# A fused Mamba-2 scan and gated feed-forward kernel: two one-element products take over waits ahead of the first state sums, and the mask products of chunk 1 are cut differently

## The chip, the core and the metric

The kernel runs on one core of a Trainium2 chip. A core has a matrix engine (TensorE, PE in the profile, with its weight loads listed as PEld), a vector engine (VectorE, DVE), an activation engine (ScalarE, ACT), a general engine (GpSimd, POOL) and an engine that issues transfers (SyncE, SP). Each runs its own list of instructions in order; they meet at semaphores. Matrix products write to PSUM, eight banks of accumulators per partition, and transfers between HBM and the on-chip memory go through 16 DMA engines.

The metric is the device time of one execution in microseconds. The kernel before has a median of 341.88 us over three runs (340.96 to 342.74).

## What is computed

A state-space scan over 4 batches, 8 heads and 768 positions, and on its output, seen as 3072 tokens of 256 features, a feed-forward block with a hard-swish gate:

```python
for c in range(nc):
    cum = np.cumsum(log_a[:, :, sl], axis=-1)
    L = np.exp(cum[:, :, :, None] - cum[:, :, None, :]) * causal
    M = np.einsum('bhin,bhjn->bhij', Cc, Bc) * L
    y[:, :, sl] = M @ xc + (Cc @ state) * np.exp(cum)
    state = decay_full * state + sum_j(Bc_j xc_j * decay_from_j)
h = x @ w_in                        # 3072 x 256 by 256 x 2048
g = h * np.clip(h + 3.0, 0.0, 6.0) / 6.0
out = g @ w_out                     # 2048 back to 256
```

The weights arrive as 64-bit floats and are turned into 32-bit ones on the chip.

## The kernel before

The sequence is cut into six chunks of 128 positions (`NC`), and each chunk into two halves of 64 (`HT`). All four batches of a chunk are done together, so a chunk is 512 tokens for the feed-forward block. The order of the work is written out by hand: the statements at the end of the kernel function are recorded in that order, each engine gets its instructions in it, and semaphore waits are put in where an instruction needs another engine's result, a transfer, or a PSUM bank that is still being read. Nothing is moved after that.

The change lies in the opening, before the first feed-forward product. In order of the program:

- `diff_mask` (L385) fills PSUM banks with the causal mask: a product of an identity matrix `ident_h` with `hide`, a 128x64 tile that is 0 where a position may be seen and a large negative number where not. For chunk 0 the four batches use banks f0 to f3, one product of 512 columns each. For chunk 1 batches 0 and 1 use the two banks "o", batches 2 and 3 the banks y0 and y1; there the bank of 8 heads is filled in 2 products for batch 0 and in 4 for the others. `mask_again` (L401) writes three of chunk 0's banks once more. These products depend only on constants and run while VectorE and ScalarE make the cumulative logarithms.
- `diff_less` (L407) and `diff_pick` (L413) add the differences of the cumulative logarithms to the masks, once VectorE has split them into three bf16 parts (L330). `diff_exp` (L422) is ScalarE's exponential of such a bank, which gives the decay matrix `L` in on-chip memory and frees the bank.
- `ends` (L451) is GpSimd's product of B with the decay at a half's end: the tile `bs`. `scores` (L569) multiplies C with B on TensorE.
- `own_banks(0)` takes the banks y0 and y1 for chunk 0's output and state sums. They held the masks of chunk 1, batches 2 and 3, so they come free with the last two exponentials of `diff_exp(1, ...)`.
- `into_state(0, 0, 1)` (L592) makes the state sums: 32 products of `bs` and `xt` in tiles of 64 rows by 32 columns (L601). The first waits for three things: a ScalarE instruction (the bank), a GpSimd instruction (`bs` of batch 0), and the transfer of `xt`, which `load_x(0)` issues on SyncE's queue at L132. An instruction carries one wait here, so the other two stand on a separate wait instruction in TensorE's list in front of it.
- `multiply(0)` copies the sums out of PSUM (`take`, L617, and L627 on ScalarE) and scales `L` by the scores on VectorE (L632). `mix(0)` (L668) makes the output of chunk 0: products of `xt` with `L` (L680) and of the state (L556). `keep(0)` copies it to `yT` (L696).
- Between these, `weights(0, n)` are pieces of the decoding of the first weights: L246, L270 and L273 on ScalarE, L249, L253, L263, L265, L277 and L287 on VectorE.
- Then `mlp_in` begins the feed-forward block of chunk 0: L706 runs 16 column blocks of two fp32 products each through four PSUM banks, with the ramp on ScalarE (L809) and its product on VectorE (L814). The later chunks use products split in three parts (L770) and follow without a pause.

An fp32 product takes two passes, each with its weight load and its product in the trace; a bf16 one takes a single pass, and its weight load is an instruction of its own in the program.

Of the kernel before, what the change touches and what calls it, by code (L numbers as in the profile page):

```python
# [21 lines left out]
def kernel(  # L22
# [24 lines left out]
    nc = tc.nc  # L47
    P = 128
    NB, NH, S, D = x.shape
# [114 lines left out]
    ident = const.tile([P, P], FP32, name="ident")  # L164
    make_identity(nc, ident)
    ident_h = const.tile([P, P], BF16, name="ident_h")
    hide = const.tile([P, HT], BF16, name="hide")
    nc.gpsimd.memset(hide, 0.0)

    def conceal_in(t, pattern):  # L170
# [23 lines left out]
        out=head, in_=head, pattern=[[-2 * N, NQ], [-N, 2]], compare_op=ALU.is_ge,  # L194
        fill=0.0, base=0, channel_multiplier=1)
    nc.gpsimd.affine_select(
        out=head, in_=head, pattern=[[2 * N, NQ], [N, 2]], compare_op=ALU.is_ge,
# [183 lines left out]
    ys, cbs, sps, adds = {}, {}, {}, {}  # L381
# [3 lines left out]
    def diff_mask(c, b):  # L385

        if c == 0:
            d = ps.tile([P, NH, HT], FP32, name="d", tag=f"f{b}")
        elif b < 2:
            d = ps_o.tile([P, NH, HT], FP32, name="d", tag="o")  # L390
        else:
            d = ps_y.tile([P, NH, HT], FP32, name="d", tag=f"y{b % 2}")
        n = NH if c else NH // (2 if b == 0 else 4)
        for h in range(0, NH, n):
            nc.tensor.matmul(  # L395
                out=d[:, h:h + n], lhsT=ident_h,
                rhs=hide.unsqueeze(1).to_broadcast([P, n, HT]), start=(h == 0), stop=True,
                skip_group_check=True)
        ds[c, b] = d
# [169 lines left out]
    def scores(c):  # L569

        bT, cT, _ = bTs[c]
        cbs[c] = [ps.tile([P, NB, 2, HT], FP32, name="cb", tag=f"f{q}") for q in range(NQ)]
        if c not in ys and c:
            own_banks(c)
        for b in range(NB):
            for a, rows in enumerate(HALF):  # L580
                for q in range(NQ):
                    pair = slice(32 * q, 32 * q + 32)
                    nc.tensor.matmul(  # L583
                        out=cbs[c][q][rows, b], lhsT=bT[pair, b, rows],
                        rhs=cT[pair, b, :, rows], start=(b == 0), stop=True,
                        tile_position=(32 * q, a * HT), skip_group_check=True)
        if c == TURN:
            from_state(c, 0)
        if 0 < c <= TURN:
            into_state(c, *range(1 if c == TURN else 2))  # L590

    def into_state(c, *halves):  # L592
        xt, bs = xts[c], bss[c]
        own = c > TURN, c >= TURN
        if c > TURN:
            sps[c][0] = ps.tile([P, NB, 2 * D], FP32, name="sp", tag="f3")
        for b in range(NB):
            for q in range(NQ):
                hs = slice(b * NH + 2 * q, b * NH + 2 * q + 2)
                for a in halves:  # L600
                    nc.tensor.matmul(  # L601
                        out=sps[c][a][32 * q:32 * q + 32, b],
                        lhsT=bs[HALF[a], hs].rearrange("s h n -> s (h n)"),
                        rhs=xt[HALF[a], hs].rearrange("s h d -> s (h d)"),
                        start=(b == 0 and (c == 0 or own[a])), stop=True,
                        tile_position=(a * HT, 32 * q), skip_group_check=True)
# [32 lines left out]
    def sums(c):  # L639

        if c < NC - 1:
            own_halves(c, 1)
            sps[c][1] = ys[c].pop("more")
        if c == TURN:
            into_state(c, 1)
            return
        into_state(c, *range(2 if c < NC - 1 else 1))
        mids[c] = att.tile([P, NB, 2 * D], FP32, name="mid", bufs=1)
        new_state(mids[c], sps[c][0], tmps[c])
# [500 lines left out]
    for c in range(2):  # L1150
        for b in range(NB):
            diff_mask(c, b)
# [49 lines left out]
    for k in range(NC):  # L1202
        gTs[k] = ffn.tile([P, NF, TB], FP32, name="gT")
        c, ahead = k + 1, k + 2
# [194 lines left out]
```

## Time and profile before

| | us |
|---|---|
| median of three runs | 341.88 (340.96 to 342.74) |
| the profiled execution | 340.38 |
| its span, from the first to the last instruction | 338.6 |
| its mean granted TensorE clock | 0.983 of full speed |

The profile is of one execution. Its page gives the busy time of each engine, the granted clock over the span, the queues of the transfers, and the chain of work that ended last; the trace behind it can be asked for the instructions of a stretch of time, for the waits of an engine, for one line or tile, and for the busy time in windows. Each waiting time is put down to the semaphore that came last by the profile's own reckoning, and "issue" stands where an engine waited for nothing that the profile knows. The duration of a matrix product is modelled; its start is measured. In a list, "x64" counts instructions that follow one another, and the time beside it covers them all.

Below is the page's second part, the span in 40 slices of 8.5 us. A digit is the busy share in tenths; PEclk is the granted clock of TensorE in tenths.

```
PE   7789999999999999999999999999999999999995
PEld 4564448888878888888888888888888888899995
DVE  7769999869789729968958657947768958599974
ACT  3858887657986752488653378634488212677661
POOL 2100000062365596269984068781048750000000
PEclk9959999999999999999999999999999999999999
DMA  6869981392990205229207239100132001110001
```

The first three slices, up to 25 us, hold the opening. TensorE has its only gaps there, apart from the very end, and in the third slice its clock is at half.

### The profile page before, as it was taken

To read this page: it belongs to the slowest core of one execution; us is meant where nothing else is said; L and a number is where in the kernel's file an instruction comes from. 1 tells how busy PE (TensorE), PEld (TensorE's weight loads), DVE (VectorE), ACT (ScalarE), POOL (GpSimd) and SP (SyncE) were. 2 spreads that over 40 slices of the span, in tenths; PEclk is the share of its full clock that TensorE was granted. 3 is DMA by queue.
4 is the path that set the end of the run, shared out by engine and by line. 5 is a ranking of instruction groups with operands and counts; after the bars stand their busy time and mean duration, and the time that the engine had idled before them with its cause. 6 is when DMAs were issued, how large, how long until landed. Compare 5 with 4: busy or idle time off the path is not lost.

```text
span 338.6 us, 8337 instructions
## 1 busy us (share of the span) xinstructions
PE 329.6 (97%) x3361; PEld 266.6 (79%) x3361; DVE 263.1 (78%) x419; ACT 208.3 (62%) x450; POOL 129.1 (38%) x126
## 2 busy tenths in 40 slices
PE   7789999999999999999999999999999999999995
PEld 4564448888878888888888888888888888899995
DVE  7769999869789729968958657947768958599974
ACT  3858887657986752488653378634488212677661
POOL 2100000062365596269984068781048750000000
PEclk9959999999999999999999999999999999999999
DMA  6869981392990205229207239100132001110001
GB/s 105 172 199 313 133 298 42 102 140 59 200 121 0 50 17 128 56 34 105 55 2 161 34 60 84 43 2 9 28 62 30 2 4 17 27 21 0 2 0 62
DMA packets 90277, 25.22 MB, mean 74 GB/s; under 512 B 82880, under 2 KB 86624, under 8 KB 89728
## 3 DMA queue, kind: packets, MB, share of 16 engines
q1 hardware_dynamic: 89664, 24.57, 38.3%
q8 instruction: 26, 0.43, 0.5%
q10 hardware_dynamic: 576, 0.13, 0.2%
q14 instruction: 11, 0.09, 0.1%
HBM read 21.33 MB, written 3.29 MB: 73 GB/s over the span
## 4 chain that ended last, share of the span: by engine, by line
PE 97%; ACT 1%; issue 0%; POOL 0%; DVE 0%; POOLq 0%
PE h L770 33%; PE wb L1018 9%; PE h L706 9%; PE wc L1018 8%; PE o L827 8%; PE wa L1018 8%; PE o_end L982 6%; PE y L680 3%; PE wb L1026 3%; PE y L556 2%; PE cb L583 2%; PE d L395 1%; PE d L417 1%; PE y L601 1%; PE d L408 1%; PE o_end L1000 1%
## 5 line engine op out<-in xcount | busy, mean ns | idle before, releaser
L814 DVE SCALAR_TENSOR_TENSOR gT<-gT,h 128x512 f32<-128x512 f32 x96 | 64.7, 683 | 22.8 <-ACT gT L809 21.4
L809 ACT ACTIVATE gT<-h,half 128x512 f32<-128x512 f32 x96 | 65.6, 685 | 25.1 <-PE h L770 21.3
L790 ACT ACTIVATE h<-h 128x512 f32<-128x512 f32 x66 | 38.2, 585 | 37.2 <-PE h L770 37.0
L770 PE MATMUL h<-y_hi,w_part 128*128 128x512 f32 x160 | 51.5, 407 | 0.0
L770 PE MATMUL h<-y_less,w_part 128*128 128x512 f32 x160 | 50.0, 399 | 0.0
L770 PE MATMUL h<-y_lo,w_part 128*128 128x512 f32 x160 | 49.5, 395 | 0.0
L873 POOL TENSOR_TENSOR s<-gT 128x512 f32<-128x512 f32 x16 | 25.3, 1583 | 50.0 <-DVE gT L814 50.0
L770 PEld LDWEIGHTS h<-y_lo,w_part 128*128 128x128 f32 x160 | 30.0, 188 | 7.3
L770 PEld LDWEIGHTS h<-y_hi,w_part 128*128 128x128 f32 x160 | 30.0, 188 | 6.9 <-DVE gT L814 0.3
L770 PEld LDWEIGHTS h<-y_less,w_part 128*128 128x128 f32 x160 | 29.1, 188 | 6.1 <-DVE h L787 0.2
L445 ACT ACTIVATE L<-L,cum_n 128x64 f32<-128x64 f32 x128 | 31.7, 337 | 1.1 <-POOL L L173 1.1
L706 PE MATMUL h<-yT,w_in 128*128 128x512 f32 x64 | 30.0, 633 | 0.0
L827 PE MATMUL o<-w_out,gT 128*128 128x256 f32 x128 | 28.8, 381 | 0.0
L827 PEld LDWEIGHTS o<-w_out,gT 128*128 128x128 f32 x128 | 24.1, 190 | 3.8 <-issue 0.5
L706 PEld LDWEIGHTS h<-yT,w_in 128*128 128x128 f32 x64 | 13.0, 205 | 16.3 <-issue 15.0
L873 POOL TENSOR_TENSOR gT<-gT 128x512 f32<-128x512 f32 x16 | 23.9, 1501 | 0.7
L173 POOL TENSOR_SCALAR_AFFINE_SELECT L<-L 64x1024 f32<-64x1024 f32 (+1 forms) x16 | 18.7, 1178 | 7.3 <-DMA L<-cum_d 7.0
L910 DVE TENSOR_TENSOR q_part<-gT,q_part 128x256 fp32r<-128x256 f32 x24 | 21.4, 922 | 0.0
L982 PE MATMUL o_end<-v_pair,g_pair 128*128 128x256 f32 x120 | 21.1, 281 | 0.0
L873 POOL TENSOR_TENSOR s<-s,gT 128x512 f32<-128x512 f32 x16 | 20.6, 1293 | 0.0
L982 PEld LDWEIGHTS o_end<-v_pair,g_pair 128*128 128x128 f32 x120 | 18.8, 189 | 1.2
L456 POOL TENSOR_TENSOR bs<-B,L 128x128 f32<-128x128 f32 x24 | 10.6, 462 | 19.3 <-ACT L L445 13.9
(166 smaller groups left out, 616.9 us busy)
## 6 DMA issues: line engine op xcount, KB each, us to landing
raw<-in_moe_w_in_dram SPq DMA_DIRECT2D x4, 1024.0 KB
raw<-in_moe_w_out_dram SPq DMA_DIRECT2D x4, 1024.0 KB
L<-cum_d SPq DMA_DIRECT2D x8, 512.0 KB
xt<-in_x_dram SPq DMA_DIRECT2D x6, 512.0 KB
out_dram<-back SPq DMA_DIRECT2D x128, 16.0 KB
B<-in_B_dram SPq DMA_DIRECT2D x6, 256.0 KB
eto<-cum_e SPq DMA_DIRECT2D x20, 64.0 KB
pairs<-in_C_dram SPq DMA_DIRECT2D x36, 32.0 KB
```

Source lines behind the costliest of these rows:

```text
L173: nc.gpsimd.affine_select(out=t[rows], in_=t[rows], pattern=pattern, compare_op=ALU.is_ge, fill=-1e5, base=base, channel_multiplier=-1)
L445: nc.scalar.activation(Ls[c][:, b, h], Ls[c][:, b, h], AF.Exp, bias=cum_n[:, c, g:g + 1])
L706: nc.tensor.matmul(out=h[:, t:t + n], lhsT=w_in[f // FP][:, j, f % FP * P:(f % FP + 1) * P], rhs=yTs[k][:, j].rearrange("p b i -> p (b i)" ...
L770: nc.tensor.matmul(out=hs_[k, f], lhsT=w[j][:, f % FP * P:(f % FP + 1) * P], rhs=y[:, j], start=(start and j == 0), stop=True, skip_group_ ...
L790: nc.scalar.activation(h, h, AF.Copy, scale=1.0 / EPS + 1.0)
L809: nc.scalar.activation(gTs[k][:, f], h, AF.Relu, bias=half, scale=1.0 / 6.0)
L814: nc.vector.scalar_tensor_tensor(out=g, in0=g, scalar=1.0, in1=h, op0=ALU.min, op1=ALU.mult)
L827: nc.tensor.matmul(out=o[:, b % 2], lhsT=gTs[0][:, f, b * P:(b + 1) * P], rhs=w_out[:, f], start=(f == 0 and b % 2 == 0), stop=True, skip_ ...
L873: nc.gpsimd.tensor_tensor(out=o, in0=p_, in1=q_, op=op)
L910: nc.vector.tensor_tensor(out=l[:, j], in0=g[:, j], in1=h[:, j].bitcast(FP32), op=ALU.subtract)
L982: nc.tensor.matmul(out=ends_["cross" if n == 2 else "squares"][b], lhsT=g_parts[t][n][:, b * P:(b + 1) * P], rhs=w, start=(t == 0 and b < ...
L1018: nc.tensor.matmul(out=bank[:, slot], lhsT=lhs[:, j], rhs=rhs[:, j], start=(clear and j == 0), stop=True, skip_group_check=True)
```

## The change

In `diff_mask` the banks of chunk 1 are filled in one product for batch 0 and in two for batch 1, where there were two and four; batches 2 and 3 keep four. This removes three weight loads and three products of TensorE's first instructions, with the same columns written.

In `into_state`, for chunk 0 alone, two products of one element each come before the sums. Both write to the first element of the bank that the sums start afresh, so their results are discarded. The first multiplies a column of `ident_h` with a column of `hide` (bf16); it is the first to write the bank, so it takes the wait on ScalarE's exponential. The second multiplies a column of `bs` with a column of `ident` (fp32); it takes the wait on GpSimd. The first state sum then has only the wait on the transfer of `xt`, and the separate wait instruction in front of it is no longer there.

```diff
@@ diff_mask
-        n = NH if c else NH // (2 if b == 0 else 4)
+        n = NH if c else NH // (1 if b == 0 else 2 if b == 1 else 4)
         for h in range(0, NH, n):
@@ into_state
         if c > TURN:
             sps[c][0] = ps.tile([P, NB, 2 * D], FP32, name="sp", tag="f3")
+        if c == 0:
+            one = sps[c][0][:1, 0, :1]
+            for left, right in ((ident_h[:, :1], hide[:, :1]), (bs[:, 0, :1], ident[:, :1])):
+                nc.tensor.matmul(
+                    out=one, lhsT=left, rhs=right, start=True, stop=True, skip_group_check=True)
         for b in range(NB):
```

TensorE's list then differs in these places alone; the lists of the other engines and the queues are the same, instruction by instruction and wait by wait:

```
before                                             after
two products d<-hide,ident_h of 256 columns        one of 512 columns
four products d<-hide,ident_h of 128               two of 256
eight products d<-hide,ident_h of 128              eight of 128
...
                                                   weight load ident_h
                                                   product y<-hide,ident_h 1x1   waits ACT
                                                   product y<-ident,bs 1x1       waits POOL
first L601, waits DMA, ACT, POOL                   first sum, waits DMA
```

## The prediction

> **What bounds the kernel now.** I read the page's busy shares and chain first, then the list of whom TensorE waited for.
>
> ```profile
> span 338.6 us, 8337 instructions
> PE 329.6 (97%) x3361; PEld 266.6 (79%) x3361; DVE 263.1 (78%) x419; ACT 208.3 (62%) x450; POOL 129.1 (38%) x126
> PE 97%; ACT 1%; issue 0%; POOL 0%; DVE 0%; POOLq 0%
> ```
>
> TensorE (PE) is busy 97% of the span and carries 97% of the chain that ends last. So time is won or lost where PE stands idle or runs slowly. The list of its waits is complete in four lines (total, times, longest):
>
> ```profile
> PE d L395 <- POOL head L192: 2.1, 1, 2.1
> PE y L601 <- ACT we L270: 1.7, 1, 1.7
> PE y L680 <- issue: 1.0, 1, 1.0
> PE y L680 <- ACT adds L617: 0.6, 1, 0.6
> ```
>
> The last three follow one another around the state sums of chunk 0, where the change is made. After them PE never waits again. Whatever moves the first up-projection product (L706) moves the end, as long as no supplier runs out. The timeline of that stretch (start, length, instruction, idle time before it and its releaser):
>
> ```profile
> 12.86 1.29 ACT L425 ACTIVATE L<-d 128x512 f32<-128x512 f32 x2 [0.31 <-PE d L417]
> 13.06 0.44 PE L417 MATMUL d<-split,pick 128*64 128x64 bf16 x16
> 15.21 1.15 ACT L273 ACTIVATE we<-we,bias_lo 128x1024 uint16<-128x1024 bf16 x1
> 15.23 0.85 PE L601 MATMUL y<-xt,bs 64*32 64x64 f32 x64 [1.73 <-ACT we L270]
> 16.27 0.35 ACT L617 COPY adds<-y 128x256 f32<-128x256 f32 x1
> 16.68 1.10 PE L680 MATMUL y<-L,xt 64*32 64x64 f32 x56 [0.59 <-ACT adds L617]
> 18.76 0.44 PE L680 MATMUL y<-L,xt 64*32 64x64 f32 x8 [0.99 <-issue]
> ```
>
> The state sums (L601) start at 15.23, although the ScalarE exponential whose PSUM bank they reuse (second L425) ended at 14.15. The profile names we L270, but the program's wait asks only for that exponential, for GpSimd's bs and for the load of x. What came last is the load of x, as the DMA columns of half-microsecond windows show (last two numbers: DMA share, GB/s):
>
> ```profile
> 14.00:14.50 0.50, 0.00 (x0) 0.00 (x0) 0.50 (x2) 0.50 (x2) 0.00 (x0) 1.00 0.09 12
> 14.50:15.00 0.50, 0.00 (x0) 0.00 (x0) 0.50 (x2) 0.50 (x1) 0.00 (x0) 1.00 0.05 8
> 15.00:15.50 0.50, 0.27 (x33) 0.30 (x34) 0.50 (x3) 0.47 (x2) 0.00 (x0) 1.00 0.00 0
> ```
>
> At 8 GB/s and a share of 0.05, about one engine of 16, something still moves between 14.5 and 15.0, and after that nothing: a straggler finishes x at about 15. The second stall is odd: 56 of 64 products of L680 run, then PE waits 0.99 us for "issue", that is, for nothing the profile knows. I looked for the instruction queue in short windows; first its line on the page, then what 16.3 to 16.5, 20.0 to 20.1 and 27.1 to 27.2 show:
>
> ```profile
> q8 instruction: 26, 0.43, 0.5%
> ...
> q8 instruction: 1, 0.02, 45.4%
> ...
> q8 instruction: 1, 0.02, 57.6%
> ...
> q8 instruction: 1, 0.02, 59.1%
> ```
>
> q8 makes 26 fetches of 0.43 MB together, 16.5 KB each; about 256 instructions if one is 64 bytes, and 26 times 256 is 6,656 against 6,722 matmul and weight-load records. The fetch at 16.3 occupies 45.4% of 16 engines over 0.2 us, or 1.45 us; the one at 20.0 takes 0.92 us and the one at 27.1 0.95 us. So the 0.99 us is TensorE's sequencer waiting for its next block of instructions.
>
> **The change part by part.**
>
> *The wait.* Before, three waits need an extra sequencer instruction, which the second row shows for L601 (shortest, median and longest of its instructions in ns, first and last start):
>
> ```profile
> L601 PEld LDWEIGHTS y<-xt,bs x64: 102/106/107, 15.2 to 15.8; 64*32 64x32 f32 x64
> ...
> L601 PEldq EVENT_SEMAPHORE  x1: 51/51/51, 15.1 to 15.1; - x1
> ...
> L706 PEldq EVENT_SEMAPHORE  x1: 51/51/51, 21.3 to 21.3; - x1
> ```
>
> It holds until 15.1 and the sequencer takes nothing further meanwhile. The next fetch appears 1.3 us after it (in the window from 16.3, at about 16.4); the one after that again 1.3 us after the stall ended at 18.76 (20.05). Counting back 256 instructions from the stall, a new block begins 13 instructions ahead of that EVENT_SEMAPHORE. I infer that a fetch starts some 15 instructions into a block, and that this wait sat just in front of that point. In the changed program it is gone: the ScalarE wait sits on a one-column bf16 product, the GpSimd wait on a one-column fp32 product (four instructions), and only the DMA wait on the first L601 product. Nothing stops the sequencer if waiting products merely queue. That they do is seen at L706: its EVENT_SEMAPHORE ran at 21.3, a microsecond before the first product it precedes, and the fetch at 27.1 belongs to a block that begins inside the sixth column block of L706, beyond the fifth, whose first product waits for the first L814 to release its bank:
>
> ```profile
> 22.34 18.00 PE L706 MATMUL h<-yT,w_in 128*128 128x512 f32 x36
> 27.77 0.68 DVE L814 SCALAR_TENSOR_TENSOR gT<-gT,h 128x512 f32<-128x512 f32 x1
> ```
>
> At 27.1 that release (28.45) had not come, yet the sequencer was past it. So with the change it passes the place while PE still works on L417, at 12.7 to 13.3, and the fetch starts 1.3 us later, at 14.0 to 14.6, instead of 16.4. The old stall ended 0.9 us after its packet (16.4 + 1.45 + 0.9 = 18.75); the same sum gives 14.0 + 0.92 + 0.9 = 15.8 to 14.6 + 1.45 + 0.9 = 17.0. PE needs the block at 17.77. The 0.99 us goes; bounds 0 (the sequencer stops at a waiting product after all) and 0.99.
>
> The Trainium skill ("Runtime: NRT & Kernel Launch", Instruction fetch mechanics) says the sequencer fetches 16 KiB blocks of 256 instructions itself while it runs the current one, and that crossing a boundary is mostly hidden. The size agrees with the 26 fetches; the hiding does not, with 0.99 us at L680, and by that rule alone this term would be 0 and the time 342.2.
>
> *What the earlier fetch costs.* It now falls on the tail of x. Fetches use one DMA engine each, and the straggler that ends x may be the engine that carried an earlier fetch. If it is the same one, x lands later by d, between 0 and 1.45 us, the longest fetch above. L601 would end at 16.08 + d, less 0.06 for the EVENT_SEMAPHORE that no longer stands between landing and weights. ScalarE is held by we L273 until 16.27 anyway, so about 0.2 us of d are covered and L680 moves by d - 0.2: from -0.06 to 1.25. I take d = 0.5, since only part of x remains at 14.3, so +0.3. Queued behind L601 are L617's copy, then L627 and L680; nobody else waits there.
>
> *The two products themselves.* Three weight loads and three passes, about 0.1 us a pair by L601's weight-load row, run at 14.15, in a gap that lasts to 15.1: 0. Without that cover they would cost about 0.3.
>
> *The merged masks.* Three weight loads and three products fewer, but the same columns:
>
> ```profile
> 2.12 3.57 PE L395 MATMUL d<-hide,ident_h 128*128 128x256 bf16 x18 [2.12 <-POOL head L192]
> 5.48 1.31 PE L403 MATMUL d<-hide,ident_h 128*128 128x512 bf16 x3
> 6.13 0.42 DVE L330 TENSOR_TENSOR split<-pre 32x256 bf16<-32x256 f32 x1
> 6.60 0.13 PEld L408 LDWEIGHTS <-split 128*128 128x128 bf16 x2 [0.54 <-DVE split L330]
> ```
>
> The 4,096 columns of L395 take 3.57 us, 0.87 ns a column, however cut; weight loads overlap. If three starts were saved it would be at most 0.1 us each, and L408 cannot start before the split at 6.55, against 6.79 now: 0, bounds -0.24 and +0.1. What the merge does is keep count: six instructions fewer ahead, six more at the sums and one EVENT_SEMAPHORE less, so all later block boundaries move by one.
>
> *Sum.* -0.99 + 0.3 + 0 + 0 = -0.7 us at L706. The profiled execution took 340.38 (span 338.6 and 1.78 around it), 1.5 less than the median 341.88 of the three runs, so I put it on both: 339.7 for that execution, **341.2** for the median.
>
> **The clock** decides how much of it arrives. Windows with the granted clock (third number from the right):
>
> ```profile
> 16.70:17.80 1.10, 1.07 (x56) 0.83 (x57) 1.07 (x3) 0.45 (x2) 0.00 (x0) 0.51 0.84 145
> 18.75:22.35 3.60, 3.59 (x105) 3.01 (x104) 1.62 (x4) 1.12 (x3) 0.64 (x1) 0.50 0.35 142
> 22.35:26.95 4.60, 4.60 (x8) 2.02 (x7) 3.44 (x8) 4.43 (x8) 0.00 (x0) 0.50 0.87 299
> 26.95:52.00 25.05, 25.05 (x60) 11.13 (x59) 23.62 (x37) 21.47 (x28) 0.00 (x0) 1.00 1.02 239
> ```
>
> After the gaps the clock is at half until 26.95, and L706 makes 8 passes in 4.60 us where PE later makes 60 in 25.05. VectorE is busy 23.62 of those 25.05 us, so its 1.43 us of slack can follow a shift of 0.7, but not one of 2 or more at once. If the clock returned at the same instant, work moved 0.7 us ahead would run at half speed and bring 0.35; if it returns in step with L706, 0.7; if sooner, more. I take 0.7, since its phase need not be the same in each run.
>
> The skill ("TensorE: Matmul & The Clock Gate", Part 1) has the gate judge free-running windows of 3.4 us, and advises no idle gap over about 3 us. The half-clock stretch of 10.2 us is three such windows, which agrees; the gap rule does not, since gaps of 1.73 and 0.59 us sufficed here.
>
> **The rivals.**
> 1. *The sequencer stops at the waiting products.* The fetch stays at 16.4, the stall remains: 341.9. For it: no row shows PE queueing past a wait on a DMA. Against it: the fetch at 27.1.
> 2. *Slower: the early fetch holds up x.* Decides from d = 1.2, where d - 0.2 eats the 0.99. With d = 1.45 L680 starts 1.25 later, PE idles 1.4 longer in the first gap, and net +0.3 is 342.2; if the clock then returns later by a third of its 10.2 us, half of 3.4 is 1.7 more: 343.9. For it: the straggler at 15 and the 1.45 us fetch. Against: it must be the same engine and the longest fetch.
> 3. *The clock comes back earlier.* A denser 16.7 to 22 could restore it before L706's 4.60 slow microseconds are over; up to half of them, 2.3, is to be had. With 1.7 more, 339.5; if x is not delayed either, 339.2.
>
> **How the numbers follow.** Forecast 0.48, rival 1 0.12, rival 2 0.15, rival 3 0.25. The forecast's own range is 340.6 to 342.0; the other cases and the spread of the runs shown (340.96 to 342.74) widen it to 338.9 to 343.3. A change under 0.5% (1.7 us) cannot be told from none here. Beyond that on the fast side lies rival 3 and a little of the forecast, 0.27; on the slow side most of rival 2, 0.12; within, 0.61.
>
> **What would show it.** Right: no EVENT_SEMAPHORE at the sums, a fetch at 14.0 to 14.6, L680's 64 products without an "issue" gap, L706 starting near 21.6. The x tail later than 15.0 would show the price. Wrong: a fetch still at 16.4, the issue gap of 1 us still there or moved elsewhere in PE's waits, or L706 not earlier than 22.3; an L408 start before 6.5 would mean that the merges count.

## The result, and the profile after

The changed kernel has a median of 338.94 us over seven runs (338.04 to 339.71) beside 341.16 us for the kernel before on the same chip (seven runs, 340.68 to 342.74). The ratio is 0.9924, with a 95% interval of 0.9901 to 0.9948. That is 2.2 us by the medians where 0.7 was forecast.

The two profiles show less of it: a span of 338.0 us against 338.6. The profile of before is of an execution of 340.38 us, below each of the seven timed runs beside it. The profile of after is of 339.71 us, the slowest of its seven. First the page and the full list of whom TensorE waited for (total, times, longest):

```profile
span 338.0 us, 8336 instructions
PE 329.5 (97%) x3361; PEld 265.8 (79%) x3361; DVE 263.0 (78%) x419; ACT 208.3 (62%) x450; POOL 130.8 (39%) x126
```

```profile
PE d L395 <- POOL head L192: 2.1, 1, 2.1
PE y L685 <- ACT adds L622: 0.8, 1, 0.8
PE y L600 <- ACT L L425: 0.7, 1, 0.7
PE y L606 <- DMA xt<-in_x_dram: 0.6, 1, 0.6
PE h L775 <- DVE gT L819: 0.5, 1, 0.5
```

The 1.0 us for "issue" is gone. The old wait of the sums is split between L600 (the new products, held by the exponential) and L606 (the sums, held by x). The timeline of TensorE there (lines behind the edit are five higher than before):

```profile
14.76 0.16 PE L600 MATMUL y<-hide,ident_h 128*1 128x1 bf16 x1 [0.69 <-ACT L L425]
14.78 0.19 PE L600 MATMUL y<-ident,bs 128*1 128x1 f32 x2
15.54 0.86 PE L606 MATMUL y<-xt,bs 64*32 64x64 f32 x64 [0.57 <-DMA xt<-in_x_dram]
17.24 0.96 PE L685 MATMUL y<-L,xt 64*32 64x64 f32 x64 [0.84 <-ACT adds L622]
...
21.33 1.22 PE L711 MATMUL h<-yT,w_in 128*128 128x512 f32 x1
```

All 64 products of L685 follow one another, and the up-projection (L711) starts at 21.33 instead of 22.34, although the work ahead of it ran about 0.6 us later in this execution (L685 starts at 17.24, L680 started at 16.68). The instruction queue in the window 14.4 to 14.6, and below it windows cut where the granted clock changes (third number from the right):

```profile
q8 instruction: 1, 0.02, 40.0%
```

```profile
17.86:21.27 3.41, 3.41 (x122) 2.90 (x104) 2.25 (x6) 1.12 (x3) 0.00 (x0) 0.50 0.61 246
21.27:24.69 3.42, 3.42 (x8) 1.51 (x5) 2.85 (x7) 3.21 (x6) 0.64 (x1) 0.50 0.48 127
24.69:52.00 27.31, 27.31 (x68) 12.69 (x67) 25.30 (x41) 22.93 (x31) 0.00 (x0) 1.00 0.98 254
```

The fetch packet of 16.38 now starts at 14.45 and takes 1.28 us (40.0% of 16 engines over 0.2 us). The clock is at half for 6.83 us instead of 10.24: two steps of 3.41 us instead of three.

This execution loses part of the lead later, at the 0.5 us of L775 above. VectorE, which the product waits for, has one slow instruction there:

```profile
98.09 1.70 DVE L747 SCALAR_TENSOR_TENSOR w_part<-w_part,w_in 128x512 fp32r<-128x512 f32 x1
99.82 0.69 DVE L750 TENSOR_TENSOR w_part<-w_part 128x512 fp32r<-128x512 f32 x1
```

In the profiles of before and of the products alone (below) the same instruction takes 0.68 us. In the run with seven fillers (below) it takes 1.71 us, and the same wait of 0.5 us is there again.

### The profile page after: what moved, and what is told of

The parts are those of the page before. It is cut to its first block, busy times and chain, and to the rows that moved or that the text cites. A ratio compares the mean times of both kernels' runs of the same rounds, so it can differ in the third digit from the quotient of the medians.

```text
span 338.0 us, 8336 instructions
## 1 busy us (share of the span) xinstructions
PE 329.5 (97%) x3361; PEld 265.8 (79%) x3361; DVE 263.0 (78%) x419; ACT 208.3 (62%) x450; POOL 130.8 (39%) x126
## 3 DMA queue, kind: packets, MB, share of 16 engines
HBM read 21.33 MB, written 3.29 MB: 73 GB/s over the span
## 4 chain that ended last, share of the span: by engine, by line
PE 82%; DVE 6%; SPq 5%; ACT 2%; POOL 2%; DMA 2%; issue 1%; POOLq 0%
PE h L775 23%; PE h L711 9%; PE o L832 8%; PE wc L1023 7%; PE wb L1023 7%; PE o_end L987 6%; PE wa L1023 6%; SPq L1054 4%; PE wb L1031 3%; PE y L685 3%; PE y L556 2%; DVE q_part L915 2%; DVE gT L819 2%; DMA xt<-in_x_dram 2%; PE cb L583 2%
## 5 line engine op out<-in xcount | busy, mean ns | idle before, releaser
L775 PE MATMUL h<-y_hi,w_part 128*128 128x512 f32 x160 | 51.7, 408 | 0.6 <-DVE gT L819 0.5
L775 PE MATMUL h<-y_less,w_part 128*128 128x512 f32 x160 | 50.0, 399 | 0.0
L775 PE MATMUL h<-y_lo,w_part 128*128 128x512 f32 x160 | 49.5, 395 | 0.0
L775 PEld LDWEIGHTS h<-y_hi,w_part 128*128 128x128 f32 x160 | 29.9, 188 | 7.9 <-DVE gT L819 1.5
L775 PEld LDWEIGHTS h<-y_lo,w_part 128*128 128x128 f32 x160 | 30.0, 188 | 7.3
L775 PEld LDWEIGHTS h<-y_less,w_part 128*128 128x128 f32 x160 | 29.1, 188 | 6.2 <-DVE h L792 0.3
L711 PE MATMUL h<-yT,w_in 128*128 128x512 f32 x64 | 29.4, 622 | 0.0
L711 PEld LDWEIGHTS h<-yT,w_in 128*128 128x128 f32 x64 | 12.7, 201 | 16.0 <-issue 13.9
L173 POOL TENSOR_SCALAR_AFFINE_SELECT L<-L 64x1024 f32<-64x1024 f32 (+1 forms) x16 | 19.5, 1229 | 8.4 <-DMA L<-cum_d 8.1
L456 POOL TENSOR_TENSOR bs<-B,L 128x128 f32<-128x128 f32 x24 | 11.7, 504 | 18.7 <-ACT L L445 12.7
```

Source lines behind the costliest of these rows:

```text
L173: nc.gpsimd.affine_select(out=t[rows], in_=t[rows], pattern=pattern, compare_op=ALU.is_ge, fill=-1e5, base=base, channel_multiplier=-1)
L711: nc.tensor.matmul(out=h[:, t:t + n], lhsT=w_in[f // FP][:, j, f % FP * P:(f % FP + 1) * P], rhs=yTs[k][:, j].rearrange("p b i -> p (b i)" ...
L775: nc.tensor.matmul(out=hs_[k, f], lhsT=w[j][:, f % FP * P:(f % FP + 1) * P], rhs=y[:, j], start=(start and j == 0), stop=True, skip_group_ ...
```

## The experiments

Each kernel was timed beside the kernel before on the same chip. The three profiles of before have no timing of their own.

| kernel | median us | ratio to before (95%) | idle at the block boundary in chunk 0's first L680, us | half clock in its profile, up to 30 us, us |
|---|---|---|---|---|
| changed kernel | 338.94 | 0.9924 (0.9901 to 0.9948) | 0 | 6.83 |
| merges alone | 341.21 | 1.0004 (0.9981 to 1.0026) | 2.9 | 10.24 |
| products alone | 339.15 | 0.9937 (0.9916 to 0.9957) | 0 | 6.83 |
| masks cut finer, 4 instructions | 340.87 | 0.9998 (0.9975 to 1.0022) | 2.2 | 10.24 |
| masks cut finer, 20 instructions | 344.02 | 1.0069 (1.0042 to 1.0095) | 1.8 | 10.24 |
| bf16 product alone | 340.78 | 0.9986 (0.9961 to 1.0010) | 2.1 | 10.24 |
| fp32 product alone | 339.93 | 0.9953 (0.9933 to 0.9974) | none listed | 10.24 |
| changed, copy four times | 340.50 | 0.9981 (0.9963 to 0.9999) | 0 | 10.24 |
| changed, 14 fillers | 340.96 | 1.0002 (0.9977 to 1.0026) | 0 | none |
| changed, 7 fillers, masks merged | 338.69 | 0.9917 (0.9890 to 0.9944) | 0 | none |

### Which part earns it

The merges alone:

```diff
@@ into_state, against the changed kernel
-        if c == 0:
-            one = sps[c][0][:1, 0, :1]
...
```

> The three merged masks alone, without the two one-element products. Theory (the place of the fetch): the EVENT_SEMAPHORE at the state sums is back, still ahead of the point at which the next instruction block is fetched, so the fetch shows at about 16.4 us again, L680 has its idle 1.0 us for nothing the profile knows, and the time is that of before (341.2 us, ratio 0.998 to 1.002). Rival (the merges earn the gain, by an earlier front part): about 338.9 us, ratio 0.993.

Nothing is gained: 1.0004. The list of waits has the old one again, larger, where the profile of before had 1.0:

```profile
PE y L680 <- issue: 2.9, 1, 2.9
```

The products alone:

```diff
@@ diff_mask, against the changed kernel
-        n = NH if c else NH // (1 if b == 0 else 2 if b == 1 else 4)
+        n = NH if c else NH // (2 if b == 0 else 4)
```

> The two one-element products alone, with the masks cut as before. Theory: no EVENT_SEMAPHORE at the state sums, the fetch at 14.0 to 14.8 us, no idle 1 us inside the first mixing products, time as the changed kernel (338.9 us, ratio 0.992 to 0.995). Rival (both parts are needed, because the merges keep the block boundaries where they were): the fetch or another one lands badly, a gap of about 1 us appears elsewhere in TensorE's waits, and the time is 340 to 341.5 us.

0.9937, all of the gain within the intervals. (The title and the text ahead of the prediction name chunk 1, which is wrong: `n = NH if c else ...` cuts the masks of chunk 0, one bank each in f0 to f3, and the banks of chunk 1 are filled in one product each. Columns, counts and places in TensorE's list are as told there, and no step depends on the chunk.) The fetch starts at 14.49 us. The merges do nothing for the time, and the six instructions by which every later block boundary moves without them cost nothing here.

### How long the old stall is

Three more profiles of the kernel before, unchanged:

> The kernel before once more, for another profile of the same program. Theory (the fetch that is asked for when x lands, 15.1 to 15.5 us, meets the weight traffic that begins at 16.3 to 16.5 us, the worse the later it is): idle time inside L680 between 1 and 3 us, depending on where x lands; half clock for 10.24 us. Rival (the stall is a constant 1.0 us): 0.9 to 1.1 us again.

> The kernel before once more, for its profile. Seven looks so far at kernels with the wait on x give idle times inside L680 of 0.99 to 2.92 us. Theory (the length of this stall spreads the times of the kernel before, one for one): idle time minus 0.99 equals the profiled execution's time minus 340.4 us, within 0.7 us. Rival (the spread comes from elsewhere): no such relation.

> As the look before: the kernel before once more, the same two expectations.

The lists of waits of the three, in that order:

```profile
PE y L680 <- issue: 1.7, 1, 1.7
```

```profile
PE y L680 <- issue: 1.9, 1, 1.9
```

```profile
PE y L680 <- issue: 1.7, 1, 1.7
```

With the profile shown ahead of the prediction, the four stalls are 0.99, 1.67, 1.91 and 1.66 us, 1.56 on average, and their executions took 340.38, 340.92, 341.33 and 340.61. Against the first, the stalls are longer by 0.68, 0.92 and 0.67 and the times by 0.54, 0.95 and 0.23, which is within the 0.7 expected; three pairs are few for a relation. (Of the seven profiles that the expectation names, five were there by then.) So the profile that the prediction was built on had the shortest stall of all.

Why the stall is longer still in most of the variants is seen when the packets are laid beside one another. Times in us from the trace; the offset is the place of the wait instruction in its block of 256, counted from the boundary at which L680 stalls:

| kernel | offset of the wait | released | fetch packet | took | first weight packet (4 KB) | idle |
|---|---|---|---|---|---|---|
| before | 13 | 15.12 | 16.38 | 1.45 | 16.40 | 0.99 |
| before, second | 13 | 15.64 | 16.88 | 1.47 | 17.09 | 1.67 |
| before, third | 13 | 15.30 | 16.57 | 1.64 | 16.54 | 1.91 |
| before, fourth | 13 | 15.22 | 16.44 | 1.74 | 16.54 | 1.66 |
| merges alone | 7 | 15.44 | 18.54 | 0.99 | 16.29 | 2.92 |
| bf16 product alone | 9 | 15.36 | 17.77 | 0.97 | 16.33 | 2.10 |
| 4 instructions more | 17 | 15.53 | 17.96 | 0.95 | 16.52 | 2.17 |
| 20 instructions more | 33 | 15.27 | 17.05 | 1.44 | 16.39 | 1.80 |
| fp32 product alone | 7 | 14.25 | 15.47 | 1.11 | 16.42 | none listed |

In five rows the packet follows the release by 1.22 to 1.27 us: where the weights' packets had not begun yet, or were just beginning. In the other four the weights were already coming by then, and the packet came 0.5 to 1.9 us later still. Among the four profiles of the kernel before this does not settle why the stall varies: the packet came after the same delay in all, it took 1.45 to 1.74 us, and the products went on 0.93, 1.48, 1.28 and 1.23 us after its end. The windows of the merges alone show how abruptly that load starts (last two numbers: DMA share, GB/s):

```profile
15.80:16.20 0.40, 0.40 (x62) 0.40 (x38) 0.40 (x2) 0.40 (x1) 0.00 (x0) 1.00 0.00 0
16.20:16.60 0.40, 0.20 (x21) 0.03 (x4) 0.40 (x2) 0.40 (x1) 0.00 (x0) 1.00 0.96 123
```

A fetch asked for when x lands runs into the load of the weights, whose first packets come 0.9 to 1.5 us after the release. That the weights delay it rests on the times alone; no run moved their load. Without the wait it is done by 15.8 us, in the lull before.

### Is it the place of the wait, or what it waits for?

The prediction held that the fetch is asked for some 15 instructions into a block, with the wait just in front. So the wait was moved behind that point, first by four instructions, then by twenty, with neither products nor merges:

```diff
@@ diff_mask, against the kernel before: four more
-        n = NH if c else NH // (2 if b == 0 else 4)
+        n = NH if c else NH // 4
@@ twenty more
+        n = NH if c else NH // (8 if b < 2 else 4)
```

> Neither products nor merges: the first mask of the second set is cut in four instead of two, which puts four more instructions ahead of the state sums, so that the EVENT_SEMAPHORE stands about three instructions behind the inferred fetch point instead of one in front of it. Theory (only the place of the wait against the fetch point counts): the fetch shows at 14 to 14.8 us although the EVENT_SEMAPHORE waits as before, the idle 1.0 us is gone, time 338.9 us (ratio 0.992 to 0.995). Rival (the products themselves matter, by spreading the waits or by keeping TensorE awake at 14.8 us): fetch and stall as before, 341.2 us.

> Neither products nor merges: the masks of the first two sets are cut in eight, 20 instructions more ahead of the state sums, so the EVENT_SEMAPHORE stands 33 instructions into its block, where the three runs in which it held back the fetch had it 7, 13 and 17 in. Theory (place of the wait against the fetch point, which lies behind the 17th instruction): the fetch shows at 14 to 15 us although the wait is there until about 15.5, no idle time for nothing inside L680, half clock for 6.83 us, 338.9 us or up to 0.5 us more where later block boundaries fall badly. Rival (any wait of the sequencer at that place costs the fetch, or the products do something else): fetch behind 16.4 us, stall, 341 us.

Both theories failed, and the fetch and the stall of the rivals came. The fetch was late with the wait at offset 17 and at 33 as well, and four instructions more gave the time of before. Twenty more made it slower, 1.0069, by far more than the 0.5 us that the theory allowed for boundaries that fall badly. The list of waits of that run has two boundaries of later chunks that had cost nothing:

```profile
PE wb L1026 <- issue: 2.2, 2, 1.1
...
PE y L680 <- issue: 1.8, 1, 1.8
...
PE d L408 <- issue: 0.5, 1, 0.5
```

All four places lie exactly where a multiple of 256 instructions ends by the prediction's count. The two at L1026 add 2.2 us and L408 0.5, beside 2.4 us by the ratio.

Then one product at a time. With the bf16 product alone the wait instruction is back and waits for x. With the fp32 product alone it is back too, but waits for the exponential:

```diff
@@ into_state, against the changed kernel: bf16 alone
-            for left, right in ((ident_h[:, :1], hide[:, :1]), (bs[:, 0, :1], ident[:, :1])):
+            for left, right in ((ident_h[:, :1], hide[:, :1]),):
@@ fp32 alone
+            for left, right in ((bs[:, 0, :1], ident[:, :1]),):
```

> The changed kernel with the bf16 product alone. It takes the ScalarE wait; the load of x and GpSimd's bs are then both left to the first state sum, and the wait on x goes to an EVENT_SEMAPHORE again, nine instructions into its block. Theory (what holds back the instruction fetch is a sequencer stopped early in a block, by whatever it waits for; only its release time counts): fetch 1.2 us or more after x has landed, behind 16.3 us, idle time for nothing inside L685 of 1 to 3 us, half clock for 10.24 us, 341 us (ratio 0.998 to 1.002). Rival (fewer waits in one instruction are what helps, or a product that keeps TensorE awake): 338.9 us.

> The changed kernel with the fp32 product alone. The EVENT_SEMAPHORE is there again, seven instructions into its block, but it waits for ScalarE's exponential (14.2 to 14.7 us), not for x. Theory (only the release time of the stopped sequencer counts): fetch 1.0 to 1.3 us after that, at 15.2 to 16.0 us, ready 0.9 to 1.45 + 0.9 us later at 17.0 to 18.3 us, where L685 needs it at about 17.6: idle 0 to 0.5 us, time 338.9 to 339.6 us, ratio 0.992 to 0.996. Rival (an EVENT_SEMAPHORE in the first instructions of a block costs the stall whatever it waits for): 341 us.

The pair tells it apart. Of the bf16 product alone:

```profile
PE y L685 <- issue: 2.1, 1, 2.1
```

Of the fp32 product alone, the wait instruction, the queue from 15.4 to 15.6, and L685:

```profile
L600 PEldq EVENT_SEMAPHORE  x1: 51/51/51, 14.2 to 14.2; - x1
```

```profile
q8 instruction: 1, 0.02, 34.7%
```

```profile
16.74 1.59 PE L685 MATMUL y<-L,xt 64*32 64x64 f32 x64 [0.59 <-ACT adds L622]
```

The fetch follows the release at 14.25 by 1.22 us, and the 64 products run through, if in 1.59 us where the products alone took 1.18. The ratio lies in the range expected, the 339.93 us a little above it. A separate wait instruction is not what costs the stall. What counts is when the sequencer that stands on it is let go. A product that keeps TensorE awake is not what helps either: the bf16 one alone runs at 14.51, and the stall is there. The fp32 product alone already keeps x's wait off that instruction, and its interval overlaps that of both products; only with both is there no such instruction at all.

### What the clock's step is worth

The changed kernel with a delay put back by hand, which no fetch has a part in:

```diff
@@ take, against the changed kernel
-        nc.scalar.copy(out=adds[c], in_=sps[c][1])
+        for _ in range(1 if c else 4):
+            nc.scalar.copy(out=adds[c], in_=sps[c][1])
```

> The changed kernel with one delay put back by hand: ScalarE copies the sums of chunk 0 to adds four times instead of once (0.35 us each), so L685 starts about 1.05 us later and TensorE idles at 16.7 to 18 us, with no instruction fetch involved. Theory A (the old stall cost its own length and, by breaking up the first half-clock step of 3.41 us, one step more at half clock): the granted clock stays at half for 10.24 us again instead of 6.83, and the time rises by 1.05 + up to 1.7 us, to 341.2 to 341.7 us, ratio to the kernel before 1.000 to 1.002. Theory B (only the length of a stall counts, the clock's return is set elsewhere): half clock for 6.83 us, time 339.7 to 340.2 us, ratio 0.996 to 0.998.

L686 (L685 there) is held for 1.68 us instead of the 0.57 of the products alone, 1.1 more. In the windows, the first half-clock step of this run, then the first two of the products alone, then the first of the kernel before (second and third number: length, PE busy):

```profile
15.63:19.04 3.41, 1.73 (x117) 1.49 (x120) 3.38 (x7) 2.90 (x7) 0.00 (x0) 0.50 0.58 161
```

```profile
16.73:20.14 3.41, 3.35 (x146) 2.90 (x148) 3.17 (x7) 1.27 (x5) 0.00 (x0) 0.50 0.86 298
...
20.14:23.56 3.42, 3.42 (x19) 2.02 (x20) 2.01 (x6) 2.68 (x6) 0.64 (x1) 0.50 0.24 46
```

```profile
16.73:20.14 3.41, 2.42 (x80) 1.93 (x80) 2.91 (x6) 0.79 (x3) 0.00 (x0) 0.50 0.86 285
```

In these three runs full clock returned after two steps in a row in which PE was busy nearly throughout. A first step with a hole in it (1.73 or 2.42 us busy of 3.41) did not count, and a third was needed. How much of a hole is too much is not settled by the busy time. The first step of the fp32 product alone did not suffice, and the second of the run with 20 instructions more, which began with 0.7 us of idle time, did:

```profile
16.67:20.08 3.41, 3.30 (x137) 2.78 (x142) 2.98 (x6) 1.29 (x5) 0.00 (x0) 0.50 0.83 282
```

```profile
19.23:22.65 3.42, 2.71 (x100) 2.26 (x99) 1.30 (x3) 0.75 (x2) 0.61 (x1) 0.50 0.23 89
```

So theory A was right on the clock, for all twelve timed runs too: their mean clocks are 0.983 to 0.985, and 10.24 us at half speed in 338 leave 0.985. The price was smaller than its 2.8 us, and the ratio of 0.9981 lies between the ranges of the two theories: 1.9 us over the changed kernel's 0.9924, 1.5 us over the 0.9937 of the products alone.

The timed runs price the step more directly. A mean clock of 0.988 or more belongs to two half steps, 0.985 or less to three. In the changed kernel and the products alone, 12 of 19 runs had two; the kernel before had none in its 35 runs beside the products alone. In those products' runs the seven with two steps have a median of 338.89 us, the five with three 339.43. By them the step is worth about 0.5 us. With the fp32 product alone four runs had two steps and eight three, with medians of 339.33 and 340.39, which is 1.1 us. These are comparisons of runs that fell one way or the other by themselves; nothing else was held fixed, so 0.5 us is no firm price.

### Holding the clock altogether

Mask products as fillers in the idle time ahead of the sums, into banks that are overwritten afterwards; first fourteen of 256 columns, then seven of 512 with all masks of `diff_mask` merged, which leaves the count of instructions ahead of the sums as in the changed kernel:

```diff
@@ into_state, against the changed kernel: 14 fillers
         if c == 0:
+            for bank, n in ((sps[c][1], 6), (sps[c][0], 8)):
+                for _ in range(n):
+                    nc.tensor.matmul(
+                        out=bank, lhsT=ident_h, rhs=hide.unsqueeze(1).to_broadcast([P, NB, HT]),
+                        start=True, stop=True, skip_group_check=True)
@@ 7 fillers (and n = NH in diff_mask, banks[c] = both in own_banks)
+            for i in range(7):
+                nc.tensor.matmul(
+                    out=banks[c][i // 4].rearrange("p a b t -> p (a b) t"), lhsT=ident_h,
+                    rhs=hide.unsqueeze(1).to_broadcast([P, 2 * NB, HT]),
+                    start=True, stop=True, skip_group_check=True)
```

> The changed kernel plus fourteen 256-column mask products into banks that are overwritten afterwards, in TensorE's idle time ahead of the state sums (13.5 to 15.1 us). They add 0.11 us each at full clock. Theory (the idle time there takes the clock down for two to three steps of 3.41 us and that decides most of what is to be had): the granted clock does not fall at 16.7 to 17.9 us, or returns a step earlier, and the time is 336 to 338 us. Rival 1 (the drop is due to the whole low use of the first 16 us, or the suppliers run out): as the changed kernel, 338.9 us. Rival 2 (the fillers end after x has landed and push the sums): slower by up to 0.5 us, 339.4 us.

> The changed kernel with seven 512-column mask products into the idle banks at 14 to 15.5 us, and all masks of chunk 0 merged, so that the number of instructions ahead of the sums is that of the changed kernel and no block boundary moves. Theory (in the run with fourteen fillers the clock held, and its gain was lost again to three fetch stalls of 2.2 us at moved block boundaries and to VectorE): clock 1.0 throughout, no L1036-like issue gaps, 336.5 to 338.3 us, ratio 0.987 to 0.992. Rival (TensorE off the half clock only runs into VectorE, 1.4 us of waits at the up-projection and more later): 338.5 to 339.5 us.

With either, the clock stays at 1.0 from 7 to 8 us to the end. The fourteen gained nothing over the kernel before: their 28 instructions moved three later boundaries into dense stretches. TensorE's waits in that run:

```profile
PE wb L1036 <- issue: 2.2, 3, 1.1
...
PE h L716 <- DVE gT L824: 1.4, 2, 0.9
```

The seven kept the boundaries in place, and the 2.2 us were gone:

```profile
PE d L395 <- POOL head L192: 2.1, 1, 2.1
PE h L717 <- DVE gT L825: 1.4, 2, 0.9
PE y L691 <- ACT adds L628: 0.5, 1, 0.5
PE h L781 <- DVE gT L825: 0.5, 1, 0.5
```

But 338.69 us is the time of the changed kernel within the intervals, so the rival's 338.5 to 339.5 holds. TensorE starts the up-projection at 19.75, 1.35 us before the products alone, and passes at full clock at once, yet at 36.1 us both are at the same product. From 30 to 40 us of this run, then of the products alone (busy times of PE, PEld, DVE, ACT, POOL):

```profile
30.00:40.00 10.00, 9.51 (x21) 3.78 (x22) 9.90 (x16) 8.49 (x11) 0.00 (x0) 1.00 1.07 154
```

```profile
30.00:40.00 10.00, 10.00 (x24) 4.37 (x23) 9.93 (x16) 8.83 (x12) 0.00 (x0) 1.00 1.21 156
```

VectorE is busy 9.9 of 10 us in both. It ends the lead, and the changed kernel is already near that limit.

## Why the prediction was right in kind and wrong in size

The step that failed is the sum. Its first term, the stall, was taken at 0.99 us and measures about 1.6; its second, the price of the earlier fetch, was taken at 0.3 and does not show; and the clock, which was let follow in step, gave some more. The forecast case had its own range from 340.6 us on, and 338.94 lies below it, at the lower edge of the wide range.

**The stall (forecast -0.99).** The mechanism held: the wait instruction is gone, the fetch started at 14.45 (forecast 14.0 to 14.6), the 64 products run without a gap, L711 started at 21.33 (forecast near 21.6). That 339.7 us was named for the profiled execution and the profile of after took 339.71 is luck: it is the slowest of seven runs and has the wait at L775. The size is where the forecast failed first. It took the 0.99 us of one profile for the stall, although that execution lay 1.5 us under the median, and did not ask whether the two belonged together. Four profiles give 1.56 us on average. The timed runs agree: 341.04 for the kernel before less 339.43 for the products alone, with the same three half steps, is 1.6.

**Its place.** That the fetch is asked for 15 instructions into a block fell: a wait at 17 and one at 33 held it as well. That a stopped sequencer holds back the fetch, and that products queued on a semaphore do not, stands: rival 1 is out, with the fetch at 14.45 while L606 waited until 15.54. The Trainium skill's sentence that a crossing is mostly hidden ("Runtime: NRT & Kernel Launch", Instruction fetch mechanics) agrees with most of the 26 fetches here and not with the 1 to 2.9 us at this one.

**The fetch on the tail of x (forecast +0.3).** Not seen. The sums started at 15.23, 15.75, 15.41 and 15.32 in the four profiles of the kernel before, and at 15.54, 15.36 and 15.53 in the changed kernel, the products alone and the run with four copies. The averages differ by 0.05 us. With this goes rival 2: what met a transfer, by the times above, was the late fetch, with the weights, and not the early one.

**The products and the masks (forecast 0 each).** Right: L600 runs at 14.76 inside the gap, and the merges alone measure 1.0004.

**The clock.** The forecast took the lead to arrive in step. It came back a step earlier in 12 of 19 runs, which is rival 3's mechanism (chance 0.25). That a hole in the first step brings the third step back is shown by the four copies, in 12 of 12 runs; why 7 of the 19 had three steps without the stall is not shown. Rival 3 priced the step at 1.7 us; it measured about 0.5 in the runs with both products. VectorE's slack, which the prediction had named with 1.43 us, may take the rest, as it does with the seven fillers; this was not measured apart. Averaged over the runs, 12/19 of 0.5 is 0.3.

So -0.99 + 0.3 should have read -1.6 + 0 and -0.3 for the clock: -1.9, where the medians show -2.2 and the interval, 0.52% to 0.99% of 341.16 us, reaches from -1.8 to -3.4.

## What to carry to other kernels

Here a wait that stood as an instruction of its own, 7 to 33 instructions into a block of 256, stopped TensorE's sequencer, and the fetch of the next block with it. Give the late semaphore to the product itself, and let small earlier products take the other waits. Before a stall is priced from one profile, compare that execution's time with the timed runs, and look again if it lies at their edge. Count instructions ahead of an edit: 20 and 28 more moved two and three block boundaries into dense stretches, at 0.2 to 1.1 us each, while 4 and 6 more cost nothing.

## What was not expected of the hardware

- A dense stretch can outrun its instructions. In the run with fourteen fillers one block's first product ran at 174.74, the fetch of the next block began at 175.69, took 0.94, and that block started at 178.04: 3.3 us for 256 instructions, with 0.9 us of idle time at the boundary.
- The clock's steps of 3.41 us have no fixed place: full clock began between 4.8 and 7.9 us in the profiles. That alone may give one program two or three half steps, which was not tried apart. The fall is plainer than the return: in all twelve profiles in which the clock fell between 15.6 and 18.5 us, PE was busy for 1.06 to 1.69 us of the step ahead of it, while a step with 1.99 (third profile of before) and those of the filled runs (2.9) kept full clock.
- How far into a block a stopped sequencer still holds back the fetch stays open: at the state sums it is beyond the 33rd instruction, and nothing was tried between that and the wait at 141 which did no harm in the changed kernel. The block before speaks against one fixed place: with merges alone the wait of L583 stands 38 instructions into it and was released at 11.08, when that block's fetch packet had begun at 10.58, and with seven fillers it stands 24 in and was released at 10.84, 0.13 us ahead of the packet.
